# A feed-forward stage rewritten as two 64-row TensorE tiles on halves of every K chunk

The program runs on one core of one Trainium2 chip. The metric is the device time of that core in microseconds (us), lower is better.

## The reference

Two blocks are computed on 2048 rows of 576 columns. Block A is windowed attention. Block B ends in a feed-forward stage, and only that stage changes:

```python
def _B_ref(x, w1, w2, w3, w4):          # x: 2048 x 576
    ...                                  # layer norm, GELU(x w1), shift of rows, w2
    x1 = x + hs
    h2 = _gelu(_layernorm(x1, axis=-1) @ w3) @ w4      # 576 -> 4608 -> 576
    return x1 + h2
...
g = _silu(_B_ref(xn, ...))
return x + s * g                         # s: the attention's result
```

576 is 4.5 chunks of 128, and 4608 is 36 chunks of 128. "Up" below is the product with w3, "down" the product with w4.

## The kernel before

The stage goes through four blocks of 512 rows. For each of 36 hidden chunks, five matmuls of 512 columns go up (K chunks of 128; the fifth is half zeros), ScalarE does the GELU, and for each of four row tiles a matmul of 512 columns (bank `pm`) and one of 64 columns (bank `pr`) come down. TensorE's order is left to the scheduler. The layer norm of the next block is issued once, at step 8, and the block is finished on VectorE while the next one begins. In the last block all up work goes first and the row tiles are finished one after another.

```python
def up(b, fc, hp):
    ph = ps_h3.tile([P, QB], FP32, name="ph3", tag="h3")          # 3 banks in turn
    for kc in range(NDC):                                         # NDC = 5
        nc.tensor.matmul(ph[:, :], lhsT=w3[:, kc, f0:f0 + P], rhs=xT_b[b % 2][:, kc, :],
                         start=(kc == 0), stop=(kc == NDC - 1))
    h3 = hp.tile([P, QB], BF16, name="h3")
    nc.scalar.activation(out=h3[:, :], in_=ph[:, :], func=ACT.Gelu_apprx_tanh)

def down(pm, pr, fc, tt):
    lhsT = h3_t[fc][:, tt * P:(tt + 1) * P]
    nc.tensor.matmul(pm[tt][:, :], lhsT=lhsT, rhs=w4[:, fc % WS, 0:M0], ...)    # 512 columns
    nc.tensor.matmul(pr[:, tt, :], lhsT=lhsT, rhs=w4[:, fc % WS, M0:D], ...)    # 64 columns

# finish of a row tile: bs = pm|pr + x1; th = tanh(bs/2) on ScalarE;
# t = bs*s; o = (th+1)*t; o = o + x -> out; g = (th+1)*bs -> DRAM   (VectorE)

for step in range(FC + LA):                                       # ... cut: b, last block
    if step < FC:
        up(b, step, h3_pool)
    if step == 8:
        for fn in ln3_steps(b + 1):                               # layer norm of the next block
            fn()
        ln3_transpose(b + 1)
    if step >= LA:
        for tt in range(TB):
            down(pm, pr, step - LA, tt)
for tt in range(TB):
    finish(b, tt, whole(tt))
```

## Time and profile before

| | before |
|---|---|
| time, median (range, runs) | 869.81 us (865.92 to 871.95, 4) |
| span of the profiled run | 863.4 us, granted clock 0.994 |
| feed-forward stage, first to last matmul start | 559.65 to 856.68, 297.0 us |
| waits of TensorE in that stage | none listed |

### The profile page before, as it was taken

To read this page: it belongs to the slowest core of one execution; us is meant where nothing else is said; L and a number is where in the kernel's file an instruction comes from. 1 tells how busy PE (TensorE), PEld (TensorE's weight loads), DVE (VectorE), ACT (ScalarE), POOL (GpSimd) and SP (SyncE) were. 2 spreads that over 40 slices of the span, in tenths; PEclk is the share of its full clock that TensorE was granted. 3 is DMA by queue.
4 is the path that set the end of the run, shared out by engine and by line. 5 is a ranking of instruction groups with operands and counts; after the bars stand their busy time and mean duration, and the time that the engine had idled before them with its cause. 6 is when DMAs were issued, how large, how long until landed. Compare 5 with 4: busy or idle time off the path is not lost.

```text
span 863.4 us, 16356 instructions
## 1 busy us (share of the span) xinstructions
PE 848.8 (98%) x6540; PEld 475.9 (55%) x6540; DVE 390.9 (45%) x1210; ACT 457.7 (53%) x819; POOL 80.7 (9%) x143
## 2 busy tenths in 40 slices
PE   8999899999999999999999999999999999999996
PEld 6665555665665665555466555544444444444455
DVE  5779731368852288871154874100053026005024
ACT  5776653598783497784378873133242333225510
POOL 3442100310100101010010102000000000000000
PEclk9999999999999999999999999999999999999999
DMA  7995741563371183382148327990023005001001
GB/s 178 247 240 135 157 85 40 132 125 70 97 125 43 53 133 84 83 156 52 13 90 156 89 67 178 325 266 1 1 79 91 1 8 153 9 1 56 1 14 45
DMA packets 138099, 83.74 MB, mean 97 GB/s; under 512 B 104497, under 2 KB 131377, under 8 KB 138017
## 3 DMA queue, kind: packets, MB, share of 16 engines
q1 hardware_dynamic: 126448, 51.24, 29.3%
q0 software_dynamic: 8448, 28.15, 11.4%
q10 hardware_dynamic: 3120, 3.25, 1.1%
q8 instruction: 53, 0.87, 0.5%
q14 instruction: 30, 0.24, 0.1%
HBM read 49.17 MB, written 9.44 MB: 68 GB/s over the span
## 4 chain that ended last, share of the span: by engine, by line

## 5 line engine op out<-in xcount | busy, mean ns | idle before, releaser
L365 ACT ACTIVATE pT<-sc 128x512 bf16<-128x512 f32 x512 | 289.5, 596 | 106.1 <-PE sc L363 98.9
L363 PE MATMUL sc<-qT,kT 128*128 128x512 bf16 x512 | 183.5, 381 | 0.8 <-DVE qT L353 0.6
L708 PE MATMUL ph<-xT_b,w_s 128*128 128x512 bf16 x720 | 172.1, 379 | 0.0
L380 PEld LDWEIGHTS <-pT 128*128 128x128 bf16 x2048 | 140.2, 98 | 54.0 <-DVE o L385 3.6
L711 ACT ACTIVATE h<-ph 128x512 bf16<-128x512 f32 x144 | 85.6, 596 | 155.6 <-PE ph L708 151.0
L380 PE MATMUL po<-v_sb,pT 128*128 128x129 bf16 x2048 | 162.7, 221 | 2.7 <-DVE o L385 2.4
L348 PE MATMUL psq<-xT_b,wq_b 128*128 128x512 bf16 x640 | 160.2, 381 | 2.3 <-DMA xT_b<-xn_b 2.0
L717 PE MATMUL pm<-w_s,h 128*128 128x512 bf16 x540 | 145.8, 380 | 0.0
L731 DVE TENSOR_TENSOR bs<-pm,x 128x512 f32<-128x512 f32 (+3 forms) x18 | 11.1, 631 | 243.1 <-PE pm L717 195.1
L404 PE MATMUL pswo<-wo_sb,oT 128*128 128x512 bf16 x512 | 116.5, 379 | 0.0
L384 DVE RECIPROCAL ri<-po 128x2 f32<-128x2 f32 x256 | 42.7, 167 | 160.2 <-PE po L380 156.8
L385 DVE TENSOR_TENSOR o<-po,ri 128x256 bf16<-128x256 f32 x256 | 107.8, 421 | 10.3 <-DMA oT<-o 4.2
L348 PEld LDWEIGHTS <-wq_b 128*128 128x128 bf16 x640 | 62.8, 98 | 77.4 <-issue 5.9
L708 PEld LDWEIGHTS <-w_s 128*128 128x128 bf16 x720 | 63.8, 98 | 73.4
L718 PE MATMUL pr<-w_s,h 128*128 128x64 bf16 x540 | 99.1, 193 | 0.0
L404 PEld LDWEIGHTS <-oT 128*128 128x128 bf16 x1024 | 65.0, 98 | 55.2
L717 PEld LDWEIGHTS <-h 128*128 128x128 bf16 x540 | 52.7, 98 | 63.8 <-issue 0.6
L355 ACT ACTIVATE qT<-psq 128x512 bf16<-128x512 f32 x96 | 57.4, 598 | 29.5 <-PE psq L348 29.5
L363 PEld LDWEIGHTS <-kT 128*128 128x128 bf16 x512 | 47.7, 98 | 28.4 <-DVE qT L353 0.9
L718 PEld LDWEIGHTS <-h 128*128 128x128 bf16 x540 | 51.0, 98 | 12.2 <-issue 0.4
L220 POOL DMA_DIRECT2D wq_b<-in_A_wq_dram x30 | 23.3, 778 | 314.1 <-PE psq L348 238.9
L414 ACT ACTIVATE s_out<-pswo 128x512 bf16<-128x512 f32 x16 | 9.6, 597 | 48.2 <-PE pswo L404 48.2
(99 smaller groups left out, 511.6 us busy)
## 6 DMA issues: line engine op xcount, KB each, us to landing
wq_b<-in_A_wq_dram POOLq DMA_DIRECT2D x30, 512.0 KB, 5.4
w_s<-in_B_w_dram SPq DMA_DIRECT2D x9, 576.0 KB, 8.5
wo_sb<-in_A_wo_dram POOLq DMA_DIRECT2D x8, 576.0 KB, 4.8
w_s<-in_B_w_dram SPq DMA_DIRECT2D x9, 512.0 KB, 9.4
x_dram<-x SPq DMA_DIRECT2D x4, 576.0 KB, 3.5
x<-x_dram SPq DMA_DIRECT2D x4, 576.0 KB, 4.6
s_b<-s_dram SPq DMA_DIRECT2D x4, 576.0 KB, 6.0
x_b<-in_A_x_dram SPq DMA_DIRECT2D x4, 576.0 KB, 6.4
```

What stands on the lines that cost most here:

```text
L348: nc.tensor.matmul(psq[:, :], lhsT=w[:, kc, hh * Dh:(hh + 1) * Dh], rhs=xT_b[qb % 2][:, kc, :], start=(kc == 0), stop=(kc == NDC - 1))
L355: nc.scalar.activation(out=qT[:, :], in_=psq[:, :], func=ACT.Copy)
L363: nc.tensor.matmul(sc[:, :], lhsT=kT[:, g, kc * P:(kc + 1) * P], rhs=qT_t[u][:, :], start=True, stop=True)
L365: nc.scalar.activation(out=pT[:, :], in_=sc[:, :], func=ACT.Exp, scale=SCALE)
L380: nc.tensor.matmul(po[:, j, :], lhsT=pTs[kc][:, tt * P:(tt + 1) * P], rhs=v_sb[:, g, kc, 0:Dh + 1], start=(kc == 0), stop=(kc == KCH - 1))
L384: nc.vector.reciprocal(out=ri[:], in_=po[:, :, Dh])
L385: nc.vector.tensor_tensor(out=o[:, t0:t0 + 2, :], in0=po[:, :, 0:Dh], in1=ri[:].unsqueeze(2).to_broadcast([P, 2, Dh]), op=ALU.mult)
L404: nc.tensor.matmul(ps, lhsT=oT_t[qb * Hq + h][:, tt, :], rhs=wo_sb[:, h, lo:hi], start=(h == 0), stop=(h == Hq - 1))
L708: nc.tensor.matmul(ph[:, :], lhsT=w3[:, kc, f0:f0 + P], rhs=xT_b[b % 2][:, kc, :], start=(kc == 0), stop=(kc == NDC - 1))
L711: nc.scalar.activation(out=h3[:, :], in_=ph[:, :], func=ACT.Gelu_apprx_tanh)
L717: nc.tensor.matmul(pm[tt][:, :], lhsT=lhsT, rhs=w4[:, fc % WS, 0:M0], start=(fc == 0), stop=(fc == FC - 1))
L718: nc.tensor.matmul(pr[:, tt, :], lhsT=lhsT, rhs=w4[:, fc % WS, M0:D], start=(fc == 0 and tt == 0), stop=(fc == FC - 1), skip_group_check=True)
```

## The change

The array is used as two tiles of 64 rows, LO (rows 0 to 63) and HI (64 to 127). Every K chunk is split in two halves, one for each tile, and the two tiles stream at the same time into different PSUM banks. 576 rows are nine halves, so two hidden chunks need nine slots of two half matmuls in place of ten full ones: no half chunk of zeros. Two tiles must not write one bank unordered: this is the rule that the prediction quotes. So each accumulation has two phases: LO writes bank 0 and HI bank 1, then they swap. Between the phases VectorE reads one element of each bank (a "fence"), and that read orders the two. The order of TensorE is fixed by hand; one GELU input of each pair is copied out by VectorE first (`hx`); `pr` becomes two banks, and `ph` has two instead of three.

```diff
-        def up(b, fc, hp):
-            for kc in range(NDC):
-                nc.tensor.matmul(ph[:, :], lhsT=w3[:, kc, f0:f0 + P], rhs=xT_b[b % 2][:, kc, :], ...)
+        def fence(lo, hi):
+            f = fence_pool.tile([1, 1], FP32, name="fence")
+            with tc.high_priority(offset=HP):
+                nc.vector.tensor_scalar(out=f[:, :], in0=lo[0:1, 0:1], scalar1=hi[0:1, 0:1], scalar2=None, op0=ALU.add)
+
+        def up(b, fc0, ps, hp, split):
+            phase1 = [lambda i=i, kc=kc: mm(i, HI if i else LO, kc, kc == 0, False)
+                      for kc in range(NDC) for i in range(2)]
+            phase2 = [lambda i=i, kc=kc: mm(i, LO if i else HI, kc, False, kc == NF - 1)
+                      for kc in range(NF) for i in (1, 0)]
+            ...  # gelu(): the second bank goes through hx, a copy on VectorE
-        def down(pm, pr, fc, tt): ...
+        def down(pm, pr, fc0, turn): ...      # half matmuls in pairs: two pm banks, two pr banks
-                for step in range(FC + LA):
-                    ...
+        with tc.manual_schedule(engines={PE}):
+                    for i in range(NP + 1):                     # NP = 18 pairs of hidden chunks
+                        if i < NP:
+                            phase1, phase2, gelu = up(b, 2 * i, ps, h3_pool, True)
+                            run(phase1)
+                            fence(*ps)
+                        if i > 0:
+                            run(down(pm, pr, 2 * i - 2, 0))
+                            fence(pm[1], pm[3])
+                        if i < NP:
+                            run(phase2)
+                            gelu()
+                        if i > 0:
+                            run(down(pm, pr, 2 * i - 2, 1))
+                            if i < NP:
+                                fence(pm[2], pm[0])
+                        if i == 4:
+                            for fn in ln3_steps(b + 1):
+                                fn()
+                            ln3_transpose(b + 1)
+                    for tt in range(TB):
+                        finish(b, tt, ...)                      # now one more read of pr for each tile
```

Cut: the load of w3, the layer norm (it now writes the last 64 columns twice, so that both halves of the array have them: four more copies of 64 columns on VectorE), the last block (the same idea, without the second turn on the down side) and the finish.

More of the change, by code (lines that the diff above doesn't have):

```diff
@@ L119, in rsqrt_table, with layernorm_steps @@
         return y
-    def layernorm_steps(pool, dsts, srcs, rsqrt=rsqrt_newton):
+    def layernorm_steps(pool, dsts, srcs, rsqrt=rsqrt_newton, twice=False):
         n = len(srcs)
@@ L138, in apply @@
         def apply(i):
-            nc.vector.tensor_scalar(out=dsts[i], in0=srcs[i], scalar1=st_["mv"][:, i, 0:1],
-                                    scalar2=st_["r"][:, i:i + 1], op0=ALU.subtract, op1=ALU.mult)
+            parts = [(dsts[i], srcs[i])]
+            if twice:
+                parts = [(dsts[i][:, 0:D], srcs[i]), (dsts[i][:, D:DP], srcs[i][:, NF * P:D])]
+            for dst, src in parts:
+                nc.vector.tensor_scalar(out=dst, in0=src, scalar1=st_["mv"][:, i, 0:1],
+                                        scalar2=st_["r"][:, i:i + 1], op0=ALU.subtract, op1=ALU.mult)
         return ([lambda i=i: stats(i) for i in range(n)] + [inv] + [lambda i=i: apply(i) for i in range(n)])
@@ L165, in ln3_steps @@
         xm = xm_b[b % 2]
-        return layernorm_steps(small, [xm[:, tt, 0:D] for tt in range(TB)], [x1_t[b][:, tt, :] for tt in range(TB)])
+        return layernorm_steps(small, [xm[:, tt, :] for tt in range(TB)], [x1_t[b][:, tt, :] for tt in range(TB)],
+                               twice=True)
     def ln3_transpose(b):
@@ L667 @@
         NSL = FC // WS
-        w3_s, w4_s = [], []
+        w3_s, w3r_s, w4_s = [], [], []
         for i in range(NSL):
-            w3_s.append(res.tile([P, NDC, WS * P], BF16, name=f"w3_s{i}"))
+            w3_s.append(res.tile([P, NF, WS * P], BF16, name=f"w3_s{i}"))
+            w3r_s.append(res.tile([P, WS // 2, P], BF16, name=f"w3r_s{i}"))
             w4_s.append(res.tile([P, WS, D], BF16, name=f"w4_s{i}"))
         h3_pool = pool("h3_pool", 6)
+        hx_pool = pool("hx_pool", 2)
         hl_pool = pool("hl_pool", FC)
@@ L675 @@
         sx_pool = pool("sx_pool", 2)
-        ps_h3 = pool("ps_h3", 3, PSUM)
+        ps_h3 = pool("ps_h3", 2, PSUM)
         ps_h2 = pool("ps_h2", 1, PSUM)
         def load_w(i):
-            w3, w4 = w3_s[i], w4_s[i]
             c0 = i * WS * P
-            nc.gpsimd.memset(w3[DR:, NF, :], 0.0)
-            nc.sync.dma_start(out=w3[:, 0:NF, :],
+            nc.sync.dma_start(out=w3_s[i][:, :, :],
                               in_=B_w3[0:NF * P, c0:c0 + WS * P].rearrange("(kc p) f -> p kc f", p=P))
-            nc.sync.dma_start(out=w3[0:DR, NF, :], in_=B_w3[NF * P:D, c0:c0 + WS * P])
-            nc.sync.dma_start(out=w4[:], in_=B_w4[c0:c0 + WS * P, :].rearrange("(fc p) d -> p fc d", p=P))
+            last = B_w3[NF * P:D, c0:c0 + WS * P].rearrange("p (j two m) -> p j two m", two=2, m=P)
+            for k in range(2):
+                nc.sync.dma_start(out=w3r_s[i][k * DR:(k + 1) * DR, :, :], in_=last[:, :, k, :])
+            nc.sync.dma_start(out=w4_s[i][:], in_=B_w4[c0:c0 + WS * P, :].rearrange("(fc p) d -> p fc d", p=P))
         with tc.issue_after(last_t[0].ins):
@@ L701 @@
         h3_t = {}
-        def up(b, fc, hp):
-            ph = ps_h3.tile([P, QB], FP32, name="ph3", tag="h3")
-            w3 = w3_s[fc // WS]
-            f0 = (fc % WS) * P
-            for kc in range(NDC):
-                nc.tensor.matmul(ph[:, :], lhsT=w3[:, kc, f0:f0 + P], rhs=xT_b[b % 2][:, kc, :],
-                                 start=(kc == 0), stop=(kc == NDC - 1))
-            h3 = hp.tile([P, QB], BF16, name="h3")
-            nc.scalar.activation(out=h3[:, :], in_=ph[:, :], func=ACT.Gelu_apprx_tanh)
-            h3_t[fc] = h3
@@ L714, in down @@
-        def down(pm, pr, fc, tt):
-            w4 = w4_s[fc // WS]
-            lhsT = h3_t[fc][:, tt * P:(tt + 1) * P]
-            nc.tensor.matmul(pm[tt][:, :], lhsT=lhsT, rhs=w4[:, fc % WS, 0:M0], start=(fc == 0), stop=(fc == FC - 1))
-            nc.tensor.matmul(pr[:, tt, :], lhsT=lhsT, rhs=w4[:, fc % WS, M0:D],
-                             start=(fc == 0 and tt == 0), stop=(fc == FC - 1), skip_group_check=True)
+        LO, HI = slice(0, P // 2), slice(P // 2, P)
+        fence_pool = pool("fence", 2)
@@ new lines, in run, with mm, gelu @@
+        def run(mms):
+            for mm in mms:
+                mm()
+        def fence(lo, hi):
[3 more added lines that the diff above has]
+        def up(b, fc0, ps, hp, split):
+            xT = xT_b[b % 2]
+            def mm(i, half, kc, first, last):
+                fc = fc0 + i
+                f0 = (fc % WS) * P
+                lhsT = w3_s[fc // WS][half, kc, f0:f0 + P] if kc < NF else w3r_s[fc // WS][half, (fc % WS) // 2, :]
+                return nc.tensor.matmul(ps[i][:, :], lhsT=lhsT, rhs=xT[half, kc, :], start=first, stop=last,
+                                        skip_group_check=True)
+            phase1 = [lambda i=i, kc=kc: mm(i, HI if i else LO, kc, kc == 0, False)
+                      for kc in range(NDC) for i in range(2)]
+            phase2 = [lambda i=i, kc=kc: mm(i, LO if i else HI, kc, False, kc == NF - 1)
+                      for kc in range(NF) for i in (1, 0)]
+            def gelu():
+                for i in range(2):
+                    src = ps[i]
+                    if i and split:
+                        src = hx_pool.tile([P, QB], FP32, name="hx")
+                        with tc.high_priority(offset=HP):
+                            nc.vector.tensor_copy(out=src[:, :], in_=ps[i][:, :])
+                    h3 = hp.tile([P, QB], BF16, name="h3")
+                    nc.scalar.activation(out=h3[:, :], in_=src[:, :], func=ACT.Gelu_apprx_tanh)
+                    h3_t[fc0 + i] = h3
+            return phase1, phase2, gelu
@@ new lines, in down_mm, with down @@
+        def down_mm(out, fc, tt, half, lo, hi, first, last):
+            return nc.tensor.matmul(out, lhsT=h3_t[fc][half, tt * P:(tt + 1) * P],
+                                    rhs=w4_s[fc // WS][half, fc % WS, lo:hi], start=first, stop=last,
+                                    skip_group_check=True)
+        def down(pm, pr, fc0, turn):
+            mms = []
+            for fc in (fc0, fc0 + 1):
+                for j in range(2):
+                    tts = (3 - j, 1 - j) if turn else (j, 2 + j)
+                    for k, half in enumerate((LO, HI)):
+                        mms.append(lambda fc=fc, tt=tts[k], half=half: down_mm(
+                            pm[tt][:, :], fc, tt, half, 0, M0, fc == 0 and turn == 0, fc == FC - 1 and turn == 1))
+                    for k, half in enumerate((LO, HI)):
+                        mms.append(lambda fc=fc, tt=tts[k], half=half, k=k, j=j: down_mm(
+                            pr[k][:, tt, :], fc, tt, half, M0, D, fc == 0 and turn == 0 and j == 0,
+                            fc == FC - 1 and turn == 1 and j == 1))
+            return mms
@@ L729, in part @@
                 bs = fin.tile([P, n], FP32, name="bs")
-                for src, l0, l1 in ps:
-                    nc.vector.tensor_tensor(out=bs[:, l0 - lo:l1 - lo], in0=src, in1=x1_t[b][:, tt, l0:l1], op=ALU.add)
+                for srcs, l0, l1 in ps:
+                    acc = x1_t[b][:, tt, l0:l1]
+                    for src in srcs:
+                        nc.vector.tensor_tensor(out=bs[:, l0 - lo:l1 - lo], in0=src, in1=acc, op=ALU.add)
+                        acc = bs[:, l0 - lo:l1 - lo]
                 th = fin.tile([P, n], FP32, name="th")
@@ L748, in finish @@
             return part
-        LA = 3
-        for b in range(NB):
-            load_sx(b)
-            lastb = b == NB - 1
-            if not lastb:
-                load_x1(b + 1)
-            pm = [ps_h2.tile([P, M0], FP32, name=f"pm{tt}") for tt in range(TB)]
-            pr = ps_h2.tile([P, TB, R0], FP32, name="pr")
-            whole = lambda tt: [([(pm[tt][:, :], 0, M0), (pr[:, tt, :], M0, D)], 0, D)]
-            if not lastb:
-                for step in range(FC + LA):
-                    if step < FC:
-                        up(b, step, h3_pool)
-                    if step == 8:
-                        for fn in ln3_steps(b + 1):
-                            fn()
-                        ln3_transpose(b + 1)
-                    if step >= LA:
-                        for tt in range(TB):
-                            down(pm, pr, step - LA, tt)
-                for tt in range(TB):
-                    finish(b, tt, whole(tt))
-            else:
-                for fc in range(FC):
-                    up(b, fc, hl_pool)
-                for tt in range(TB - 1):
-                    for fc in range(FC):
-                        down(pm, pr, fc, tt)
-                    finish(b, tt, whole(tt))
-                tt = TB - 1
-                part = finish(b, tt, [])
-                cuts = [0, 288, 480, D]
-                for i in range(3):
-                    lo, hi = cuts[i], cuts[i + 1]
-                    ps = pm[TB - 1 - i][:, 0:hi - lo]
-                    for fc in range(FC):
-                        nc.tensor.matmul(ps, lhsT=h3_t[fc][:, tt * P:(tt + 1) * P],
-                                         rhs=w4_s[fc // WS][:, fc % WS, lo:hi], start=(fc == 0), stop=(fc == FC - 1))
-                    part([(ps, lo, hi)], lo, hi)
@@ new lines @@
+        NP = FC // 2
+        with tc.manual_schedule(engines={PE}):
+            for b in range(NB):
+                load_sx(b)
+                if b < NB - 1:
+                    load_x1(b + 1)
+                    pm = [ps_h2.tile([P, M0], FP32, name=f"pm{tt}") for tt in range(TB)]
+                    pr = [ps_h2.tile([P, TB, R0], FP32, name=f"pr{i}") for i in range(2)]
+                    n2 = None
+                    for i in range(NP + 1):
+                        if i < NP:
+                            ps = [ps_h3.tile([P, QB], FP32, name="ph3", tag="h3") for _ in range(2)]
+                            phase1, phase2, gelu = up(b, 2 * i, ps, h3_pool, True)
[16 more added lines that the diff above has]
+                    for tt in range(TB):
+                        finish(b, tt, [([([pm[tt][:, :]], 0, M0), ([p[:, tt, :] for p in pr], M0, D)], 0, D)])
+                    continue
+                pend = None
+                for i in range(NP + 1):
+                    nxt = None
+                    if i < NP:
+                        if i % 3 == 0:
+                            ps = [ps_h3.tile([P, QB], FP32, name="ph3", tag="h3") for _ in range(2)]
+                        else:
+                            ps = [ps_h2.tile([P, QB], FP32, name=f"pm{2 * (i % 3) - 2 + k}") for k in range(2)]
+                        nxt = up(b, 2 * i, ps, hl_pool, False)
+                        run(nxt[0])
+                        fence(*ps)
+                    if pend:
+                        run(pend[1])
+                        pend[2]()
+                    pend = nxt
+                cuts = [(tt, 0, D) for tt in range(TB - 1)] + [(TB - 1, 0, 288), (TB - 1, 288, 480), (TB - 1, 480, D)]
+                part = None
+                for i, (tt, lo, hi) in enumerate(cuts):
+                    pa = [ps_h2.tile([P, M0], FP32, name=f"pm{2 * (i % 2) + k}") for k in range(2)]
+                    pr = [ps_h2.tile([P, TB, R0], FP32, name=f"pr{k}") for k in range(2)] if hi - lo > M0 else None
+                    hm = min(hi, lo + M0)
+                    for fc in range(FC):
+                        for k, half in enumerate((LO, HI)):
+                            down_mm(pa[k][:, 0:hm - lo], fc, tt, half, lo, hm, fc == 0, fc == FC - 1)
+                        if pr:
+                            for k, half in enumerate((LO, HI)):
+                                down_mm(pr[k][:, tt, :], fc, tt, half, M0, D, fc == 0, fc == FC - 1)
+                    srcs = [([p[:, 0:hm - lo] for p in pa], lo, hm)]
+                    if pr:
+                        srcs.append(([p[:, tt, :] for p in pr], M0, D))
+                    if lo == 0:
+                        part = finish(b, tt, [])
+                    part(srcs, lo, hi)
```

## The prediction

> **What bounds the kernel now.** I read the page's first two parts, then the groups by form, then the feed-forward stage in order of time on TensorE, then VectorE around one block end.
>
> ```profile
> PE 848.8 (98%) x6540; PEld 475.9 (55%) x6540; DVE 390.9 (45%) x1210; ACT 457.7 (53%) x819; POOL 80.7 (9%) x143
> ...
> PE   8999899999999999999999999999999999999996
> ...
> DVE  5779731368852288871154874100053026005024
> ```
>
> TensorE is busy in every slice. The stage that changes is the last third: its first up-projection matmul starts at 559.7 us and its last matmul ends near 857. VectorE is nearly idle there except for three bursts and the end.
>
> ```profile
> L708 PE MATMUL ph<-xT_b,w_s 128*128 128x512 bf16 x720 | 172.1, 379 | 0.0
> L717 PE MATMUL pm<-w_s,h 128*128 128x512 bf16 x540 | 145.8, 380 | 0.0
> L718 PE MATMUL pr<-w_s,h 128*128 128x64 bf16 x540 | 99.1, 193 | 0.0
> ```
>
> 720 matmuls of 512 columns go up, 540 of 512 and 540 of 64 come down, and none of them waited (0.0). The means (379, 193 ns) are latencies; what a matmul costs in a stream is the distance between starts:
>
> ```profile
> 603.10 0.38 PE L717 MATMUL pm<-w_s,h 128*128 128x512 bf16 x1
> ...
> 603.31 0.19 PE L718 MATMUL pr<-w_s,h 128*128 128x64 bf16 x1
> ...
> 603.34 0.38 PE L717 MATMUL pm<-w_s,h 128*128 128x512 bf16 x1
> ```
>
> A 512-column matmul takes 0.216 us, a 64-column one about 0.029 us with its weight load. A step (one 128-wide hidden chunk) is 9 x 0.2157 + 4 x 0.029 = 2.058 us; 144 steps make 296 us, which is the stage. It is pure streaming, so only fewer or shorter streams can help, and any new wait on TensorE is lost time.
>
> The third view is VectorE where a block of 512 rows ends (its output is finished while the next block begins):
>
> ```profile
> 707.58 1.29 DVE L731 TENSOR_TENSOR bs<-pm,x 128x512 f32<-128x512 f32 x2 [52.68 <-PE pm L717]
> 708.79 0.35 DVE L731 TENSOR_TENSOR bs<-pr,x 128x64 f32<-128x64 f32 x2
> 709.05 0.75 DVE L735 TENSOR_TENSOR t<-bs,s_b 128x576 f32<-128x576 f32 x1
> 709.75 0.76 DVE L741 SCALAR_TENSOR_TENSOR g<-th,bs 128x576 bf16<-128x576 f32 x1
> ...
> 717.17 0.22 DVE L731 TENSOR_TENSOR bs<-pr,x 128x64 f32<-128x64 f32 x1
> ```
>
> The last read of the old block's pr bank is at 717.4, 9.8 us after the first finishing operation. TensorE doesn't notice: there the scheduler has moved it on to 20 up matmuls in a row and put the 64-column ones off until 717.44. The reader should remember that this freedom of order hides the 10 us.
>
> **What the Trainium skill says.** "TensorE: Matmul & The Clock Gate", Back-to-back issue gap: N/2.4 + 2.5 ns between warm matmuls; that is 215.8 and 29.2 ns, and the trace agrees (216, 29). Same page, Part 3 (Packing small matmuls): matmuls on different row groups run side by side, about 4 ns apart. No run here shows it yet. "TensorEngine Tiling (Array Packing)", Gotcha 1: row tiles cannot access the same PSUM bank at the same time, software must synchronise; hence the hand-over. "TensorE" again, Architectural detail: VectorE and ScalarE are strict first-in-first-out. The trace before agrees as far as it shows: VectorE runs one operation after another, each after what it waits for.
>
> **The change part by part.**
>
> Streams. 576 rows are 4.5 chunks of 128, and the kernel before pays 5, half a chunk of zeros. With 64-row halves, two hidden chunks need 18 half matmuls, 9 slots instead of 10. 72 pairs x 0.2157 = 15.5 us saved, if two tiles really stream at once. Down keeps its slots (each full one becomes two halves side by side). TensorE gets 3672 matmuls in this stage instead of 1908.
>
> Extra in the short slots. A 64-column slot now needs two weight loads and two matmuls in 29 ns. The 29 ns rhythm before shows one load plus matmul fits, not two. My estimate is 0 to 29 ns more per slot, 540 slots: 0 to 15 us; I take 10 ns, some 4 us after waits that it fills.
>
> Hand-over waits. Between phase 1 and 2 of each accumulation VectorE must read both banks. Chain: matmul latency past its slot 0.16 us, 0.04 to VectorE, a tiny operation 0.16 to 0.17 (as the 128x2 reciprocal), 0.055 back to TensorE (714.52 to 714.575): about 0.43 us. The work put in between is 0.86 us (phase 2), 0.98 (half of down) or 1.08 (phase 1), so in an undisturbed pair fences are hidden. The bank release is tighter: gelu on ScalarE (0.596) and, in parallel, a 128x512 copy on VectorE (0.687 for the like cast of qT), with 0.2 before and 0.055 after, about 0.95 to 1.0 against 0.98. I take 0.03 us for each of some 38 pairs: 1.2 us. There is 1.3 us at the start, where nothing stands between phases.
>
> But the fences leave only 0.4 to 0.6 us of room, TensorE's order is now fixed by hand, and VectorE has other work. In the built program I followed VectorE's queue row by row with the durations above:
> - Layer norm of the next block stands among four hand-overs in blocks 0 to 2: in the trace before, stats take 3.8 us, the Newton steps 2.2, applying 1.4, now with four 64-column copies more 1.9. The four TensorE waits come to 1.13 + 1.17 + 1.59 + 0.38 = 4.3 us, three times: 12.8 us.
> - Block ends 0-1 and 1-2: the first fence stands behind six finishing operations (wait 1.6 us), the copy of the first pair behind four more (1.7), and the first down matmuls need every pr read, now 8 reads instead of 4 and a copy and two fences in the same queue. The last lies about 11.6 us after the block's end, while TensorE is there after 3.2 (14 up slots and one pm). With the next fence behind three more operations: about 9 us each, 18 us.
> - The last pair of a block has no up work between its two down halves: 2 x 0.34, three times: 2 us.
> - Block end 2-3: up matmuls want pm banks that are still read, 5.7 us, and a rotation wait for gelu, 1.1: 6.8 us.
> - Last block: both pr banks are single, so cuts 2 and 3 each wait for the finishing reads (about 1.6), the first for the last gelu: 3.5 us. At the very end one more addition per part and 0.5 us of order: 0.7 us.
>
> Sum: -15.5 + 4 + 1.2 + 1.3 + 12.8 + 18 + 2 + 6.8 + 3.5 + 0.7 = +34.8; about 0.5 us of waits before go, so +34: 869.2 + 34 = **903 us**.
>
> **The rivals.**
>
> Rival 1, the intended gain: tiles stream side by side and the waits are small, because VectorE is only 45% busy. Then 869.2 - 15.5 + 3 = 857. For it: the 98% streaming stage and the skill's 4 ns. Against it: the average hides that VectorE's 10 us bursts stand ahead of the fences in a first-in-first-out queue. Even complete, it gives 1.8%, so faster by over 2% is nearly closed.
>
> Rival 2, the tiles do not overlap well: weight loads of half height are slower or cannot be pulled ahead past a waiting matmul. With 29 ns more in each short slot, 912; if loads showed in every slot (say 30 ns x 1188 wide slots more), 940; if pairs ran one after the other, above 1100. Against it: loads of 128 columns fit 29 ns in the trace before, and a wide slot has 216.
>
> Rival 3, TensorE idles long enough that its clock drops: the longest single wait I find is 3.4 us at block end 2-3. It would add a few us only.
>
> **Range and chances.** My own sum without any extra in the short slots is 899, with all of it 912. Waits may be off by a third (15 us) either way; serial tiles are a small tail upwards. Range 886 to 924. Faster by over 2% (below 851.8): 0.02. Within 2% (to 886.6): 0.14. Slower: 0.84.
>
> **What would show it.** Right: in the steady part of a block two half matmuls of a pair start some ns apart and pairs 0.216 us, a pair of hidden chunks takes about 3.9 to 4.0 us instead of 4.12; TensorE's groups show idle time before them ended by VectorE fences, hx or bs, gathered in about 4 us per layer norm and 9 us per block end; TensorE's digits fall to 5 to 8 in three or four slices; idle in all about 45 us. Wrong: a steady pair well over 4.12 us means that tiles do not overlap (rival 2); block ends without gaps mean that VectorE's queue was not what TensorE waits for, and about 857 (rival 1). A lower granted clock after 559 us would mean rival 3.

## More of the kernel before

The prediction quotes the page's shares, the three groups of the stage, the steady rhythm and the VectorE burst at a block end. One more line matters for what follows. It is the windows view of the kernel before for the 20 us in which block 0 is finished: stretch, length, then busy time of PE, PEld, DVE, ACT, POOL, the granted clock, DMA share and GB/s.

```profile
640.00:660.00 20.00, 19.99 (x131) 9.67 (x130) 12.81 (x39) 7.01 (x12) 0.00 (x0) 1.00 0.59 167
```

VectorE is busy for 12.81 of 20 us, and TensorE for 19.99: the burst costs nothing here.

## The result

| | before | after |
|---|---|---|
| time, median (range, runs) | 869.81 us (865.92 to 871.95, 4) | 910.93 us (903.66 to 920.12, 4) |
| profiled run: span, granted clock | 863.4 us, 0.994 | 901.9 us, 0.978 |
| stage, first to last matmul start | 297.0 us | 331.9 us |

The ratio is 1.045, interval 1.0373 to 1.0528: slower. All ratios here are the mean time of one kernel's fast runs over that of the other's fast runs of the same rounds, so they are not quite the ratio of the medians quoted. The run of 920.12 us was slow (clock 0.969) and is left out of the ratio. The results are correct.

The page of the changed kernel, to be laid beside the lines in the prediction:

```profile
PE 846.7 (94%) x8225; PEld 498.9 (55%) x8304; DVE 470.7 (52%) x1478; ACT 459.2 (51%) x819; POOL 76.6 (8%) x134
...
PE   8999899999999989999999999899789969997996
...
DVE  5869731668731759831448830443753375336134
...
PEclk9999999999999999999999999999799979999998
```

A slice is 22.5 us here, and the stage begins with the 26th digit. Its full slices are lost where the prediction put them: the 8 there holds the start of the stage and the first two waits of the first layer norm, the 7, the 6 and the 7 that follow are the three block ends, and the 8 between the first two of them is the second layer norm; the third shows no lower digit. The granted clock falls to 7 in the slices of the first two block ends. VectorE's average went from 45% to 52%, which says nothing yet.

First the part that worked: the steady stretch in TensorE's order of time (start, us, engine, line, operation, count).

```profile
602.29 0.40 PE L753 MATMUL pm<-w_s,h 64*128 64x512 bf16 x2
602.51 0.21 PE L753 MATMUL pr<-w_s,h 64*128 64x64 bf16 x2
602.53 0.40 PE L753 MATMUL pm<-w_s,h 64*128 64x512 bf16 x2
```

Each row is now a pair (x2), and the rows start where those of the kernel before did: 0.22 us from a wide to a narrow one, then 0.02 to 0.03. From one wide pair to the next it is 0.245 us, as 0.216 + 0.029 before. So the two tiles stream side by side, and a narrow slot with twice the matmuls and weight loads costs nothing extra.

Where the time went is in the view of who waited, TensorE alone, from 560 to 902 us (engine, what it was to write, releaser: us in total, times, longest):

```profile
PE pr L753 <- DVE bs L783: 8.0, 8, 2.0
PE ph L731 <- DVE hx L745: 6.4, 6, 1.5
PE ph L731 <- DVE fence L722: 5.8, 6, 1.4
PE pm L753 <- DVE fence L722: 5.0, 10, 0.9
PE pm L731 <- DVE bs L783: 4.6, 3, 3.0
```

The kernel before has no such line. Every releaser here is VectorE; the view's two lines left out are 0.5 us for VectorE and 0.2 for ScalarE. That view counts from the modelled end of the matmul before, and gives about 30 us. Counted by a script from start to start in tile LO by itself, less the slot's own length, the waits longer than 0.15 us sum to 40.4 us in 40 places.

The first end of a block, on TensorE; brackets give the wait and its releaser:

```profile
642.11 1.04 PE L731 MATMUL ph<-xT_b,w_s 64*128 64x512 bf16 x8 [1.45 <-DVE fence L722]
644.63 2.46 PE L731 MATMUL ph<-xT_b,w_s 64*128 64x512 bf16 x8 [1.48 <-DVE hx L745]
...
648.81 0.21 PE L753 MATMUL pr<-w_s,h 64*128 64x64 bf16 x1 [0.86 <-DVE bs L783]
651.05 0.21 PE L753 MATMUL pr<-w_s,h 64*128 64x64 bf16 x1 [2.04 <-DVE bs L783]
```

And VectorE in the same time:

```profile
639.60 0.69 DVE L783 TENSOR_TENSOR bs<-pm,x 128x512 f32<-128x512 f32 x1 [1.22 <-PE pr L753]
...
641.86 0.20 DVE L722 TENSOR_SCALAR fence<-ph,ph 1x1 f32<-1x1 f32 x1
...
643.89 0.68 DVE L745 COPY hx<-ph 128x512 f32<-128x512 f32 x1
...
650.78 0.22 DVE L783 TENSOR_TENSOR bs<-pr,bs 128x64 f32<-128x64 f32 x1
```

The fence takes 0.20 us but starts at 641.86, behind six operations of the finish that began at 639.60; TensorE starts again at 642.11. The copy `hx` stands behind four more. The last read of the old `pr` bank begins at 650.78, 11.2 us after the first operation of the finish, and TensorE's next narrow matmul waits for it until 651.05. The same two windows as before and around the drops of the clock:

```profile
600.00:620.00 20.00, 20.00 (x256) 11.16 (x254) 6.60 (x20) 6.15 (x10) 0.00 (x0) 1.00 0.01 2
...
640.00:660.00 20.00, 14.16 (x124) 6.12 (x121) 16.06 (x38) 6.20 (x10) 0.00 (x0) 0.74 0.47 149
...
670.50:674.80 4.30, 2.18 (x25) 0.96 (x23) 3.88 (x19) 0.80 (x2) 0.00 (x0) 1.00 0.00 0
674.80:678.20 3.40, 3.40 (x24) 2.03 (x22) 1.73 (x8) 0.43 (x1) 0.00 (x0) 0.50 0.60 116
```

In the undisturbed 20 us TensorE is as full as before with VectorE busy for a third of it. At the block end VectorE is busy 16.06 of 20 us and TensorE only 14.16. The clock went to half five times, for 30.7 us in all, each time just after such waits; 43 slots of LO ran through at half clock, which cost 8.4 us (44 slots and 8.8 us in HI).

The whole budget of the stage, worked out from the starts of the trace: the streams (count of matmuls by their pitch, two half matmuls to a slot) are 296.6 us before and 281.1 after, so the saving of 15.5 us is there. What is beyond the streams is 0.4 us before and 50.8 after: in LO 40.4 in the waits, 8.4 at half clock, and the remaining 2.0 in gaps below 0.15 us (in HI 40.0, 8.8 and 2.2). 50.8 - 0.4 - 15.5 = 34.9 us, the growth of the stage from 297.0 to 331.9.

### The profile page after: what moved, and what is told of

Its sections match the earlier page's. It is cut to its first block, busy times and chain, and to the rows that moved or that the text cites. A ratio compares the mean times of both kernels' runs of the same rounds, so it can differ in the third digit from the quotient of the medians.

```text
span 901.9 us, 20226 instructions
## 1 busy us (share of the span) xinstructions
PE 846.7 (94%) x8225; PEld 498.9 (55%) x8304; DVE 470.7 (52%) x1478; ACT 459.2 (51%) x819; POOL 76.6 (8%) x134
## 4 chain that ended last, share of the span: by engine, by line
PE 82%; DVE 11%; DMA 3%; issue 2%; ACT 1%; SPq 0%; DVEq 0%; ACTq 0%
PE pm L753 14%; PE psq L353 13%; PE pswo L409 12%; PE ph L731 12%; PE po L385 11%; PE sc L368 10%; PE pm L731 3%; PE ph L457 2%; DMA xnnT<-xnn_b 2%; PE psx L508 2%; DVE ln_st L132 2%; PE pswr L409 2%; PE pr L753 1%; DVE bs L783 1%; DVE qT L358 1%
## 5 line engine op out<-in xcount | busy, mean ns | idle before, releaser
L753 PE MATMUL pm<-w_s,h 64*128 64x512 bf16 (+3 forms) x1296 | 165.4, 361 | 5.6 <-DVE fence L722 5.0
L353 PE MATMUL psq<-xT_b,wq_b 128*128 128x512 bf16 x603 | 151.9, 379 | 3.7 <-DMA xT_b<-xn_b 1.6
L753 PEld LDWEIGHTS <-h 64*128 64x128 bf16 x2376 | 101.9, 96 | 82.1 <-issue 23.5
L731 PE MATMUL ph<-xT_b,w_s 64*128 64x512 bf16 x960 | 134.5, 386 | 12.5 <-DVE hx L745 6.4
L753 PE MATMUL pr<-w_s,h 64*128 64x64 bf16 x1080 | 118.5, 191 | 8.0 <-DVE bs L783 8.0
L747 ACT ACTIVATE h<-ph 128x512 bf16<-128x512 f32 x66 | 38.9, 597 | 145.5 <-PE ph L731 144.2
L731 PEld LDWEIGHTS <-w_s 64*128 64x128 bf16 x1152 | 62.8, 96 | 71.1 <-issue 27.7
L722 DVE TENSOR_SCALAR fence<-pm,pm 1x1 f32<-1x1 f32 x117 | 24.5, 209 | 67.8 <-PE pm L753 50.9
L745 DVE COPY hx<-ph 128x512 f32<-128x512 f32 x54 | 37.3, 691 | 35.4 <-PE ph L731 35.4
L722 DVE TENSOR_SCALAR fence<-ph,ph 1x1 f32<-1x1 f32 x60 | 12.5, 208 | 79.6 <-PE ph L731 79.6
```

The lines of the kernel that those rows point to most:

```text
L353: nc.tensor.matmul(psq[:, :], lhsT=w[:, kc, hh * Dh:(hh + 1) * Dh], rhs=xT_b[qb % 2][:, kc, :], start=(kc == 0), stop=(kc == NDC - 1))
L731: return nc.tensor.matmul(ps[i][:, :], lhsT=lhsT, rhs=xT[half, kc, :], start=first, stop=last, skip_group_check=True)
L745: nc.vector.tensor_copy(out=src[:, :], in_=ps[i][:, :])
L747: nc.scalar.activation(out=h3[:, :], in_=src[:, :], func=ACT.Gelu_apprx_tanh)
L753: return nc.tensor.matmul(out, lhsT=h3_t[fc][half, tt * P:(tt + 1) * P], rhs=w4_s[fc // WS][half, fc % WS, lo:hi], start=first, stop=last, ...
```

## The experiments

Theory A: each time, TensorE waits because a hand-over (fence, `hx` or a bank's last read) stands in VectorE's queue behind work that has no hurry: the next layer norm, and the finish of the block. Rivals: the fence itself costs too much, whatever stands before it (B); VectorE is the wrong engine for it (C); the lost clock is the main loss (D); row tiles were needed for nothing but the half chunk (E). The expectations letter some of these otherwise: their C is the throttle (D here), their E the engine of the fence (C here), their F the change of tile shape (E here), and their D says that two tiles side by side are themselves slower. All kernels computed correct results. The runs of the first four and of the last three share a chip and the runs of the kernel before.

| kernel | median us (range, runs) | ratio to before [95%] | stage us |
|---|---|---|---|
| before, beside the first four | 864.63 (863.33 to 873.99, 7) | 1 | 297.0 (first profile) |
| ln_spread | 889.20 (882.48 to 891.25, 4) | 1.0247 [1.0165, 1.0328] | 317.0 |
| early_release | 888.64 (883.79 to 893.67, 4) | 1.0281 [1.0208, 1.0355] | 316.8 |
| both | 874.76 (870.95 to 886.87, 4, one slow) | 1.0073 [0.9986, 1.0160] | 300.9 |
| pipelined | 860.08 (853.39 to 865.40, 4) | 0.9927 [0.9837, 1.0017] | 285.4 |
| before, beside the last three | 865.09 (863.33 to 873.99, 8) | 1 | |
| scalar_fence | 923.70 (916.58 to 926.86, 4) | 1.0657 [1.0567, 1.0747] | 340.7 |
| half_chunk_only | 867.76 (865.35 to 871.06, 4) | 1.0018 [0.9945, 1.0091] | 298.1 |
| pipelined_again | 859.78 (856.08 to 861.03, 6) | 0.9918 [0.9868, 0.9968] | 285.4 |

The changed kernel was not run again beside the experiments; its times are those of the result above. The stage (first up matmul to last matmul of one profiled run each) is the better measure of the two: it leaves out the attention stage, whose length varied between profiles by more than some of the effects.

### Layer norm in pieces

The layer norm is cut into 13 parts (4 statistics, 4 Newton parts, 4 applications, 1 transpose), and each part is issued behind the first fence of one pair. All fences stay.

```diff
-                        if i == 4:
-                            for fn in ln3_steps(b + 1):
-                                fn()
-                            ln3_transpose(b + 1)
+                            if i == 3:
+                                ln_q += ln3_steps(b + 1, parts_=True)
+                                ln_q.append(lambda b=b: ln3_transpose(b + 1))
+                            if i >= 4:
+                                pop(ln_q, f)          # one part, issued after this pair's fence
```

> The changed kernel, with the next block's layer norm cut into 13 pieces, each queued on VectorE behind a different pair's first fence; nothing else moved. Theory A (TensorE waits because other VectorE work stands ahead of fences in a first-in-first-out queue): the four waits of 1.06 + 1.11 + 1.34 + 0.68 = 4.2 us per block shrink to under 0.3, so 12 us less in all, and 1 to 3 us of half-clock time beside them go too: about 893 against some 906 of the changed kernel. The block ends keep their waits. Rival B (the hand-over by a fence costs what it costs, whatever else VectorE does): the time stays within 3 us of the changed kernel.

Measured: the stage took 317.0 us, 14.9 less than the changed kernel's 331.9. In the changed kernel VectorE's queue at the first layer norm reads so:

```profile
583.31 0.77 DVE L132 BATCH_NORM_STATS2 ln_st<-x 128x6 f32<-128x288 bf16 x2
583.99 0.19 DVE L722 TENSOR_SCALAR fence<-ph,ph 1x1 f32<-1x1 f32 x1
...
588.62 1.73 DVE L143 TENSOR_SCALAR xn_b<-x,ln_mv,nr_y 128x576 bf16<-128x576 bf16 x6
590.25 0.20 DVE L722 TENSOR_SCALAR fence<-pm,pm 1x1 f32<-1x1 f32 x1
```

The last fence sits behind six applications of 1.73 us. With the parts spread no wait over 0.2 us is left between 575 and 630 us; in the view of who waited in that run, the line of the narrow matmuls is what it was, and that of `hx` has fallen from 6.4 to 3.7 us:

```profile
PE pr L776 <- DVE bs L806: 8.0, 8, 2.1
...
PE ph L754 <- DVE hx L768: 3.7, 3, 1.5
```

So the layer norm was worth about 15 us: by the same count in LO, 12.3 of them are waits and 2.1 the half clock (6.3 us left of 8.4). The block ends are another matter.

### Banks read first

At the end of a block all reads of its banks go first, and the other 16 operations of the finish are issued one for each pair of hidden chunks, behind its `hx` copy. The layer norm stays where it was. Two more edits came with this one, here and in the next two kernels: the GELU outputs get 36 buffers in place of 6, and the store of `g` goes through another DMA queue. The changed kernel's TensorE waited for a GELU once, 0.2 us, so the gain is not from there.

```diff
+        def release(b, pm, pr):
+            bss = [bs_pool.tile([P, D], FP32, name="bs") for _ in range(TB)]
+            with tc.high_priority(offset=HP):
+                for tt in (0, 2, 1, 3):
+                    nc.vector.tensor_tensor(out=bss[tt][:, 0:M0], in0=pm[tt][:, :], in1=x1_t[b][:, tt, 0:M0], op=ALU.add)
+                    if tt == 2:
+                        ...                            # the eight reads of pr
+            for tt in range(TB):
+                fin_q.extend(finish_steps(b, tt, bss[tt]))      # popped one a pair
-                    for tt in range(TB):
-                        finish(b, tt, ...)
+                    release(b, pm, pr)
```

> The changed kernel, with only the block end changed: all reads of the old block's banks come first on VectorE (four buffers for the sums), the other 16 finishing operations are queued one per pair behind the hx copy. Theory A: of 8 to 9 us of waits per block end about 4.5 stay (fence behind the reads 2.7, copy 1.0, last pair 0.7), so 15 us less, and the clock drops of 10 us at block ends 0-1 and 1-2 vanish, 4 to 5 us more: about 887. Layer norm waits stay at 4.2 us each. Rival B: within 3 us of the changed kernel. Rival C (the throttle, not the waits, is the main loss): the gain is over 25 us, because the long idle stretches are gone.

Measured: 316.8 us, 15.1 less than the changed kernel. The waits of `pr` fell from 8.0 to 2.2 us (all four that are left lie in the last block), and the layer norm's stayed (1.06, 1.10, 1.33 and 0.67 us in the first block):

```profile
PE ph L733 <- DVE fence L723: 9.0, 6, 2.6
...
PE pr L755 <- DVE bs L828: 2.2, 4, 0.7
```

The longest wait is now one of a fence, 2.6 us: on VectorE it stands behind the twelve reads that were put first, which began at 635.42.

```profile
638.88 0.20 DVE L723 TENSOR_SCALAR fence<-ph,ph 1x1 f32<-1x1 f32 x1
```

Half of the block end's loss is moved, not removed. Of the 15.1 us, by the count in LO, 11.2 are waits and 3.6 the half clock. The expectation that the clock drops of the block ends vanish held for one of the two: the drop at 640.0 us stayed, for 6.8 us.

### Both

Both edits, and the last block's second pair of `pr` banks taken from `ps_h3`.

```diff
-                    pr = [ps_h2.tile([P, TB, R0], FP32, name=f"pr{k}") for k in range(2)] if hi - lo > M0 else None
+                    if hi - lo > M0 and i % 2 == 0:
+                        pr = [ps_h2.tile([P, TB, R0], FP32, name=f"pr{k}") for k in range(2)]
+                    elif hi - lo > M0:
+                        pr = [ps_h3.tile([P, TB, R0], FP32, name="pr_b", tag="h3") for k in range(2)]
```

> Layer norm spread, early release, and in the last block two sets of banks in turn for the 64-column remainder. Theory A: the gains add up, 12 + 15 + 3.2 for the last block, and all clock drops vanish (6 to 7 us): about 870, like the kernel before, with the two-tile stream's 15.5 us eaten by some 14 us of waits that are left (start 1.3, steady 0.5, last pair 2, block ends 9, first cut 0.9). Rival B: within 5 us of the changed kernel.

Measured: 300.9 us, 31.0 less than the changed kernel; the single gains were 14.9 and 15.1. The sum is near 31.0, but the third edit has its share: the last block's four waits for the old `pr` reads, 3.1 us in the changed kernel, are gone. So the first two gave 27.9 together. Their waits do add up (40.4 - 12.3 - 11.2 - 3.1 = 13.8 us; 14.4 are left), so these are two separate losses with the same cause; the clock does not (2.7 us would be left, it is 4.0, in two stretches of half clock of 3.4 and 6.8 us where the expectation had none). The time is level with the kernel before (the interval holds 1). Beyond the streams there are 300.9 - 281.1 = 19.8 us left, 9.6 of them waits where VectorE reads the banks at block ends (the longest is 2.6 us, a fence).

### Pipelined across blocks

The next block's first pair goes up between the two down turns of the last pair, so work stands where the block ends had none; the reads of two `pm` banks move to ScalarE; the eight narrow reads become two; fences go ahead of the reads; the last block starts on the banks that have been free longest.

```diff
-                for tt in (0, 2, 1, 3):
-                    nc.vector.tensor_tensor(out=bss[tt][:, 0:M0], in0=pm[tt][:, :], in1=x1_t[b][:, tt, 0:M0], op=ALU.add)
+                for tt in (2, 3):
+                    nc.scalar.activation(out=bs[:, tt, 0:M0], in_=pm[tt][:, :], func=ACT.Copy)
+                dve(0); rest(); dve(1)        # rest(): both pr banks, [128, 4, 64] at a time
...
-                    for i in range(NP + 1):
-                        if i < NP:
-                            phase1, phase2, gelu = up(b, 2 * i, ps, hl_pool, True)
+                    for i in range(1 if b else 0, NP + 1):
+                        phase1, phase2, gelu = up(b + i // NP, 2 * (i % NP), ps, hl_pool, True)
```

> As both, and the first pair of the next block goes up between the two down halves of the last pair (no neighbouring phases left), the banks are read by ScalarE and VectorE together, fences get the highest priority, and the last block's cuts start on the banks that are free longest. Theory A: waits left are about 4 us in all (start 1.3, about 1 per block end, steady 0.5), so the two-tile stream shows nearly its whole 15.5 us: 856 to 862, 1.0 to 1.5% faster than the kernel before. If two tiles side by side were themselves slower than one (rival D: short slots or weight loads), it would not get below 866.

Measured: 285.4 us, 46.5 less than the changed kernel and 11.6 less than the kernel before. These are several edits at once, and no run separates them. The page's first line:

```profile
PE 831.3 (97%) x8225; PEld 494.6 (58%) x8304; DVE 466.8 (54%) x1461; ACT 460.7 (54%) x825; POOL 76.3 (9%) x134
```

VectorE is at 54% of the span, more than in the changed kernel (52%), for nearly the same work in less time: in the stage alone it is busy for 147.4 of 285.6 us, before for 150.8 of 332.1, with 177 fences in both and 55 `hx` copies for 54. The view lists a wait for it only at the start of the stage; by the starts, block ends still cost 0.8, 0.8 and 0.2 us. A run of the same kernel with more rounds gives the view of who waited:

> The same kernel as pipelined, five rounds, because its gain of 0.7% had an interval from -1.6 to +0.2%. Theory A expects the feed-forward stage at 285 to 286 us again, 11.5 us under the kernel before, and a ratio of 0.983 to 0.993; the attention stage, which is the same in all these kernels, moves by some us from run to run.

```profile
PE ph L755 <- DVE hx L769: 0.8, 1, 0.8
PE ph L755 <- DVE fence L745: 0.3, 1, 0.3
```

Its ratio is 0.9918 [0.9868, 0.9968], the stage 285.4 us again. So this version is faster than both kernels, by 0.8%, which is within 2%. Of 11.6 us saved in the stage some 5 reach the medians (4.6 and 5.3), and 6 to 7 by the ratios. The rest is open: the stage began between 557.8 and 571.0 us in the profiles of the different kernels, although the order of the attention stage's instructions is the same on every engine; the ones that began late waited more before it, but not in one place (in the pipelined profile TensorE waited 3.4 us for the transposed layer-norm tile `xnnT`, in those of before and of the second pipelined run not at all). One profile of each is not enough to tell a cost of the change from a difference between runs.

### The fence on ScalarE

```diff
-                nc.vector.tensor_scalar(out=f[:, :], in0=lo[0:1, 0:1], scalar1=hi[0:1, 0:1], scalar2=None, op0=ALU.add)
+                for x in (lo, hi):
+                    nc.scalar.activation(out=f[:, :], in_=x[0:1, 0:1], func=ACT.Copy)
```

> The changed kernel with each fence read by ScalarE (two 1x1 copies) in place of VectorE. Theory A (what counts is VectorE's queue against a fixed order of TensorE, not which engine fences): nothing is won. The layer norm now holds up the hx copy in one piece, about 4.5 us per block where four fence and copy waits made 4.2; block ends still wait for the reads of pr; two ScalarE reads between gelus add about 0.1 us to each of 54 pairs. So 5 to 15 us slower than the changed kernel, feed-forward stage 336 to 345 us against its 332. Rival E (VectorE fences are the fault, a less loaded engine mends it): 20 us faster or more.

Measured: slower than the changed kernel, stage 340.7 us against 331.9. The waits for fences fell from 10.8 us to 7.0 (two lines of the view below), and those for `hx` rose from 6.4 to 17.8:

```profile
PE ph L732 <- DVE hx L746: 17.8, 7, 4.8
...
PE ph L732 <- ACT fence L723: 3.6, 3, 1.6
PE pm L754 <- ACT fence L723: 3.4, 6, 0.7
```

VectorE in that kernel at the first layer norm:

```profile
590.13 0.81 DVE L132 BATCH_NORM_STATS2 ln_st<-x 128x6 f32<-128x288 bf16 x2
...
596.18 2.28 DVE L143 TENSOR_SCALAR xn_b<-x,ln_mv,nr_y 128x576 bf16<-128x576 bf16 x8
598.37 0.69 DVE L746 COPY hx<-ph 128x512 f32<-128x512 f32 x1
```

The layer norm runs through without a break for 8.2 us, and the one hand-over still on VectorE stands behind all of it. So another engine for the fence does not mend it (rival C): what stands before a hand-over counts. The test is not a pure one, since ScalarE needs two reads for each fence.

### The half chunk alone

From the kernel before: only the two half chunks of a pair of hidden chunks run as 64-row tiles, each into its own bank. No fence, no `hx`, no fixed order; the layer norm's four more copies are in it.

```diff
+            for i, ph in enumerate(phs):                      # after four full chunks for each of two hidden chunks
+                half = slice(i * DR, (i + 1) * DR)
+                nc.tensor.matmul(ph[:, :], lhsT=w3r_s[fc0 // WS][half, (fc0 % WS) // 2, :], rhs=xT[half, NF, :],
+                                 start=False, stop=True, skip_group_check=True)
```

> The kernel before, with row tiles for nothing but the half chunk: four full chunks each for two hidden chunks, then the two half chunks side by side, each into its own bank, so that no bank is handed over and no fence, no hx copy and no fixed order are needed. It saves the same 72 x 0.216 = 15.5 us of streaming, but changes the tiling mode twice per pair. The one change from full to half tiles in the trace of the changed kernel took 126 ns where 29 were due, about 0.1 us lost. Theory F (each change of mode drains the array, 0.1 us): 144 x 0.1 = 14 us are given back, 863 to 870 us, stage about 295. If changes were free: stage 282, 850 us. If a change back costs more than that (0.2 us each): stage 310.

Measured: 298.1 us and a ratio of 1.0018: nothing gained, though TensorE waits for nobody. TensorE's order of time shows why:

```profile
601.10 1.24 PE L715 MATMUL ph<-xT_b,w_s 128*128 128x512 bf16 x5
602.28 0.39 PE L719 MATMUL ph<-xT_b,w3r_s 64*128 64x512 bf16 x2
602.60 0.39 PE L729 MATMUL pm<-w_s,h 128*128 128x512 bf16 x1
```

The two halves do start together, and the next full matmul starts 0.319 us after them, where a slot is 0.216: 0.103 us lost. The last full one before them started at 601.967, 0.311 us ahead: 0.095 lost. With the 4 ns between the two halves it is 0.202 us (also the mean of the 66 pairs whose records are complete), and 72 pairs make 14.5 us, which nearly eats the 15.5; another 2 us or so, in smaller gaps, were not followed up. So rival E fails: the change of tile shape costs as much as it saves unless the whole stage stays in one shape, which is what the change did.

### What was not run

The author reports that a version without fences, and one with fences whose TensorE order is left to the scheduler, were built, and that the race check of both found two row tiles writing one bank without an order between them. Neither was run: take it as not shown. What the free order of the kernel before would hide in this form stays open.

## Why the prediction was right

It said 903 us, slower, for waits behind VectorE's queue. It came to 910.93, in the range.

- **Streams, -15.5 us.** Right: 296.6 to 281.1 us by the starts in the trace.
- **Short slots, +4 us.** Wrong in size: a wide and a narrow pair still take 0.245 us. This term measured 0.
- **Layer norm, 4.3 us for each.** Right: 1.06, 1.11, 1.34 and 0.68 us in block 0 (of the two tiles, the one that waited less), 4.2 in sum, against 1.13, 1.17, 1.59 and 0.38 predicted; in blocks 1 and 2 about 3.7 and 3.1. Spreading it took out 14.9 us for three, 12.8 predicted: 12.3 of waits, and 2.1 of the lost clock, which followed two of the three.
- **Block ends, 9 us each.** The places are right (first fence, copy, narrow matmuls, in that order), the waits are 7.1 and about 8.0 us, a little under the predicted size; the half clock that begins in them adds its own loss, which the prediction did not have. Block end 2-3: 5.1 us for 6.8. The last read lies 11.2 us after the first, 11.6 predicted.
- **Last pair of a block, last block, start.** 0.9 us for 0.68 each, 3.5 for 3.5, 1.4 for 1.3.
- **The clock.** This was rival 3, "a few us only", and not in the sum. It measured 8.4 us, and mostly not by one long wait as that text had it: the drop at 674.8 us came after waits of at most 1.2 us as that view lists them. Only the one at 821.6 us followed a long one (3.0).

In sum: -15.5 + 0 for the short slots + 42.4 for waits and gaps (40.4 + 2.0, where the prediction's terms make 45.6 without the span's end) + 8.4 for the clock is 35.3, less the 0.4 of gaps before: 34.9 for the stage, where the prediction had 34.8 with the span's end. The mechanism and the places were right; that the sums agree so closely is luck: 4 us too much for the short slots and 3 too much for the waits stand against 8.4 for the clock, which was left out. One sum of the prediction is off by itself: 29 ns more in each of 540 short slots is 15.7 us on 899, so 915 and not 912. The profiled spans differ by 38.5 us: 34.9, 2.3 of a later start of the stage and 1.3 at the end. The later start was not predicted, and is in the open part named above.

Of the rivals, 1 (small waits) and 2 (no overlap of tiles) are refuted by the waits and by the pitch. Rival B falls with the pipelined version, where the same number of fences costs next to nothing; what is true of it is about 4 us in the changed kernel (1.4 at the start, 2.7 in the three last pairs), where no TensorE work covers a hand-over. D falls by size: 8.4 of 50.8 us, and the clock came back (0.994) once the waits were gone.

## What to carry to other kernels

When TensorE's order is fixed and its banks pass through another engine, that engine's queue is on the path: look at what stands ahead of each hand-over, not at the engine's average busy share, which was higher in the fastest version than in the slow one (the same work in a shorter time). Read the banks first, cut all background work into pieces shorter than the slack of a hand-over, and put TensorE work of the next block where the last one ends. Row tiles save stream time in full when a whole stage runs in them; to switch for a single half chunk gives the gain back.

## What the Trainium skill lacked or had wrong

- "TensorE: Matmul & The Clock Gate", Part 3 (Packing small matmuls), has about 4 ns between the starts of matmuls on different row groups. Here it is 2 to 4 ns in the half-chunk kernel (602.278 and 602.282 us), where both start after a change of tile shape, and 3 to 4 ns in the first five pairs of the changed kernel's stage. Later in its streams of pairs it is mostly 10 to 20 ns, and about 200 ns in 219 of the 1836 pairs. That costs nothing: each tile still keeps its own 0.216 us.
- The same page, Part 1, puts the drop to half clock after about one idle window of 3.4 us. Here it dropped with TensorE busy for 2.18 of the 4.30 us before, and no listed wait over 1.2 us. (Its passage on PSUM-queue cycling allows for frequent short idles, without a figure.) The layer norm of block 0, with nearly the same waits, brought no drop. The lengths of the half-clock stretches (3.4 and 10.2 us, one and three times 3.4) agree with the window, and the five drops lie 9, 17, 8 and 18 times 3.413 us apart. In the 3.413 us before each drop, by the starts, TensorE streamed for 26, 40, 41, 37 and 6% of the time; cut into the same steps, the emptiest at block 0's layer norm has 42%. So what seems to count is how empty such a step is, and so where its limits fall. It is not a sharp limit: in the kernel with banks read first, steps with 38 and 40% brought no drop.
- "TensorEngine Tiling (Array Packing)", Key Properties, says that a change of tiling mode drains TensorE, without a figure: 95 ns going in and 103 ns coming out between 512-column matmuls.
- The same page, Gotcha 1, asks software to synchronise the banks, without a cost: a 1x1 read of both banks takes 0.19 to 0.21 us on VectorE, and where nothing stood before it and no TensorE work beside it, the last pair of block 0 waited 0.45 us for each.
